# Replacing a hand-placed instruction order by a build-time list scheduler in a fused memory-attention and gated-MLP kernel

## The chip, the cores and the metric

The kernel runs on one core of one Trainium2 chip. The metric is device time in microseconds (us). The profile records the span from the first to the last instruction, which in these runs is 1.7 us shorter than the time. Engine names: PE is the TensorE matmul unit, PEld its weight loads, DVE is VectorE, ACT is ScalarE, POOL is GpSimd, SP is the engine that here only issues DMAs. The program gives each engine its own list of instructions; "order" in this text means the order of that list, engine by engine. That an engine keeps to it shows in the trace of the kernel before: from 95.71 to 96.65 us DVE stood idle, waiting for an ACT result, although the matmuls of two k groups were done at 94.4 us and only had to be copied out by DVE; these copies came later in its list.

An execution has a state, fast or slow (slow when it is more than 1.5% above the fastest of its kernel).

## The reference, cut to what matters

The input x is 2048 tokens of 512 values, in four segments of 512 tokens. Two branches read it and a gate per token mixes them.

```python
g = sigmoid((x * gate_w).sum(-1))                       # one gate per token
# branch A: 32 heads of 16, causal softmax inside each segment, plus a memory of earlier segments
for s in range(4):
    p = softmax(q_s k_s^T / 4 + causal_mask); a_dot = p @ v_s
    a_mem = (phi(q_s) @ M) / (phi(q_s) @ z + 1e-6)      # phi(t) = t + 1 if t > 0 else exp(t)
    o_s = sigmoid(beta) * a_mem + (1 - sigmoid(beta)) * a_dot
    M += phi(k_s)^T v_s ; z += phi(k_s).sum(tokens)
a = concat(o) @ wo
# branch B: gated MLP, width 1792
b = (gelu(x @ w_gate) * (x @ w_up)) @ w_down
out = g * a + (1 - g) * b
```

## The kernel before: the parts that the argument touches

There are three stages. First the inputs load and segment 0's k, q and v are computed. Then the gate matmuls of the MLP run with Gelu on ACT. Then comes the logit stage: 80 "logit slots" (4 segments, 4 chunks of 8 heads, 5 slots each). Each slot is a few small matmuls into two of three PSUM buffers called `lg`, followed by two exps of 128x1024 on ACT. All other PE work is "filler" between slots: k, q and v of the next segment, up projections, down and output projections, the PV products (`pv`) and the memory. Each filler group uses one of only two PSUM buffers called `gen`, which an "evacuation" by DVE (or ACT) must empty before it can be used again. The kernel has no other PSUM (matmul result memory) buffers than these five, before and after the change.

The order of filler work is written by hand. A running total of nominal PE costs spreads it over the slots, and a queue `pend` hands out small DVE operations one at a time:

```python
def qk_group(s, c, which):                   # filler: one k or q group
    t = gen(which)
    ...4 matmuls into t...
    nc.vector.tensor_copy(dst, t[:, :])                          # evacuation, DVE
    if which == "k":
        nc.vector.tensor_scalar_mul(KO[...], dst, odd[:, :])     # kO: SBUF to SBUF, DVE

def phi(src, dst):                           # phi of a 128x1024 tile
    nc.scalar.activation(E, src, AF.Exp)
    nc.vector.tensor_scalar_max(Q1, src, 0.0)
    nc.vector.tensor_scalar_min(E, E, 1.0)
    nc.gpsimd.tensor_add(dst, E, Q1)                             # POOL, 2.15 us

# ... fillers of segments 1 and 2 (cut):
f += [fl(0, phi_k, s, 0)] + f_k(s + 1, 0) + f_num(s, 1) + f_q(s + 1, 0)
f += f_out(s - 1, 0) + f_num(s, 2) + f_m(s, 0) + f_v(s + 1) + f_out(s - 1, 1)
# ...
for t in range(NSLOT):                       # per segment
    logit_slot(s, t)
    target = total * (t + 1) / NSLOT
    while True:
        if pvq and pvq[0][0] <= g and not opened:
            pv_group(*pvq.popleft()[1:]); pump(1); continue
        if not fs or done >= target:
            break
        cost, opened, fn = fs.popleft()
        fn(); done += cost; pump(1)
```

At the start, the small operations on `beta` (`bps`, a matmul into a `gen` buffer, and `tb`, an ACT operation) come before everything else in program order, and the tiny transfers gw and beta are issued on ACT's queue right after wk.

The softmax here doesn't subtract the row's maximum and nothing guards it: scores larger than these inputs give would overflow.

## Time and profile before

Before: 336.63 us median over 15 runs (335.74 to 338.76).

| stage (from the profile) | us | length, us |
|---|---|---|
| start, up to the first gate matmul | 0 to 29.0 | 29.0 |
| gates, up to the first exp | 29.0 to 93.7 | 64.7 |
| logit stage, first exp to end of last exp | 93.7 to 325.0 | 231.3 |
| tail | 325.0 to 337.3 | 12.3 |

These lines are from the profile page of the kernel before: the span, each engine's busy time, and the span in 40 equal slices, where each digit is the busy share in tenths (PEclk is the clock granted to PE).

```profile
span 337.3 us, 5732 instructions
PE 291.8 (87%) x2297; PEld 120.0 (36%) x2297; DVE 224.4 (67%) x425; ACT 200.0 (59%) x208; POOL 121.3 (36%) x186
PE   1389999999949997896899799869979998999963
DVE  1265354455585889789766886995787698456473
ACT  0122555344466786786478487828785686797840
PEclk9999999999987999999599899969998999999999
```

No engine is full throughout the last 70% of the span, although PE looks nearly so. The Trainium skill, "Perfetto Trace Analysis", section "Identifying the Most-Contended Engine", says that matmul busy share is not a good measure of how close PE is to its limit. This trace agrees: PE's busy time is larger than what its instructions need, as the next view shows. It gives the busy time of each engine in the logit stage of the kernel before; after the length come PE, PEld, DVE, ACT and POOL, then granted clock, DMA share and GB/s.

```profile
core 0: us, PE busy (x) PEld busy (x) DVE busy (x) ACT busy (x) POOL busy (x), PEclk, DMA share, GB/s
93.73:325.02 231.29, 206.87 (x1914) 83.22 (x1912) 174.32 (x330) 165.16 (x172) 114.84 (x171) 0.94 0.06 15
```

PE is "busy" for 207 us here, but the same instructions need about 187 us at full clock (an estimate: columns streamed at the trace's 0.216 us per 512, plus 0.1 us for each change to or from the small packed matmuls). The granted clock of 0.94 says where part of the difference lies.

The timeline of the start of the kernel before; columns are start, duration, engine, line, operation, output<-inputs, count, and in brackets the idle time before it and what ended it.

```profile
6.57 0.46 ACTq L89 DMA_DIRECT2D wq<-in_A_wq_dram  x1
12.64 1.28 ACT L184 ACT_TABLE_LOAD   x1 [12.64 <-DMA xT<-in_A_x_dram]
13.93 0.17 ACT L184 ACTIVATE tb<-bps 128x4 f32<-128x4 f32 x1
14.15 1.87 PE L150 MATMUL k<-xT,wk 128*128 128x512 bf16 x4 [5.37 <-ACT tb L184]
```

PE waited 5.4 us for `tb`, which held one of the two `gen` buffers, and ACT reached `tb` only after it had issued all its weight loads. The four matmuls then took 1.87 us; they began 0.43 us apart, where later ones begin 0.216 us apart.

The timeline of two stalls early in the logit stage of the kernel before:

```profile
96.99 0.69 DVE L157 CAST kT<-k 128x512 bf16<-128x512 f32 x1
97.22 2.12 POOL L330 TENSOR_TENSOR pkT<-E,Q 128x1024 bf16<-128x1024 bf16 x1 [1.07 <-issue]
97.71 1.78 DVE L161 TENSOR_SCALAR kO<-kT,odd 128x512 bf16<-128x512 bf16 x1
97.73 1.02 PE L150 MATMUL q<-xT,wq 128*128 128x512 bf16 x4 [3.35 <-DVE kT L157]
99.41 0.68 DVE L157 CAST kT<-k 128x512 bf16<-128x512 f32 x1
100.14 1.86 PE L150 MATMUL q<-xT,wq 128*128 128x512 bf16 x4 [1.05 <-DVE kT L157]
```

`kO` takes 0.35 us alone (at 100.12 in the same trace). Here it took 1.78 us and ended at 99.49, just after POOL's add ended at 99.34. The Trainium skill, "SBUF — State Buffer", section "Who interferes with whom", says that certain DVE operations and POOL exclude each other for a whole instruction; the trace agrees with that. The second kT evacuation waited behind it, and PE waited 1.05 us for the evacuation. The longer stall just before, 3.35 us, has nothing to do with POOL: the first kT evacuation stood in DVE's list behind phi's operations, and these waited for phi's exp, which ACT reached only at 95.56, after two exps of logits. At about 98.95 us the granted clock fell to 0.50 (1.00 in the window 98.8 to 98.9, 0.50 in 99.0 to 99.1), and the four matmuls at 100.14 took 1.86 us instead of 1.02. The second stall began only at 99.09, so it was not the one that brought the clock down here.

Three lines of the list of waits of the kernel before (who waited for whom: us in total, times, longest) show PE's largest wait and what such waits do to ACT:

```profile
PE q L150 <- DVE kT L157: 5.3, 6, 3.3
ACT pT L280 <- PE lg L276: 33.2, 44, 2.5
ACT pT L280 <- PE lg L269: 22.2, 11, 6.3
```

ACT, which needs about 155 us for the 160 exps (an estimate from the 1.94 us that two take back to back), waited 55 us for logits. PE itself waited 22.9 us for DVE evacuations in the logit stage (the sum of its lines in that list).

### The profile page before, as it was taken

The page shows a single profiled execution, that of the slowest core. Times are in us where ns is not written, and L with a number is a line of the kernel's source. Part 1 is how long each engine was busy: PE and PEld are TensorE (multiplying, and loading weights), DVE is VectorE, ACT ScalarE, POOL GpSimd, SP SyncE. Part 2 cuts the span into 40 slices and gives each one's busy share as a digit, 9 for nine tenths or more (in the row PEclk, how much of TensorE's full clock was granted, in tenths as well). Part 3 has the DMA queues.
Part 4 walks back from the last instruction along what each step waited for, and adds up shares of the span by engine and source line. Part 5 has one row for each costly group of instructions (what it writes and reads, how often), then busy time and mean ns, then how long its engine had stood idle before and what let it go on. Part 6 is the DMA issues. An engine that isn't in the chain of part 4 may idle for free.

```text
span 337.3 us, 5732 instructions
## 1 busy us (share of the span) xinstructions
PE 291.8 (87%) x2297; PEld 120.0 (36%) x2297; DVE 224.4 (67%) x425; ACT 200.0 (59%) x208; POOL 121.3 (36%) x186
## 2 busy tenths in 40 slices
PE   1389999999949997896899799869979998999963
PEld 0034444444413443342243343314424343334321
DVE  1265354455585889789766886995787698456473
ACT  0122555344466786786478487828785686797840
POOL 6000000000045345555255564346464533454520
PEclk9999999999987999999599899969998999999999
DMA  7999400000000001000100100010010000000001
GB/s 141 241 272 342 157 1 0 2 0 0 2 16 16 3 0 33 2 2 2 31 16 4 46 16 17 1 33 17 2 31 18 32 2 2 16 17 31 4 2 63
DMA packets 23108, 13.75 MB, mean 41 GB/s; under 512 B 16168, under 2 KB 22056, under 8 KB 23080
## 3 DMA queue, kind: packets, MB, share of 16 engines
q1 hardware_dynamic: 20400, 9.97, 10.9%
q10 hardware_dynamic: 2680, 3.41, 3.5%
q8 instruction: 18, 0.29, 0.4%
q14 instruction: 10, 0.08, 0.1%
HBM read 7.60 MB, written 2.10 MB: 29 GB/s over the span
## 4 chain that ended last, share of the span: by engine, by line
PE 65%; DVE 22%; ACT 5%; SPq 2%; issue 2%; DMA 2%; ACTq 0%; POOLq 0%; POOL 0%; DVEq 0%
PE gt L211 14%; PE up L175 14%; PE out L402 9%; PE lg L276 5%; PE v L166 4%; PE q L150 4%; PE dn L402 3%; PE pv L300 3%; DVE kO L161 3%; PE out L407 3%; DVE T L307 2%; DVE kT L157 2%; SPq L84 2%; DVE osb L425 2%; ACT pT L280 2%
## 5 line engine op out<-in xcount | busy, mean ns | idle before, releaser
L280 ACT ACTIVATE pT<-lg 128x1024 bf16<-128x1024 f32 x160 | 153.4, 1024 | 56.2 <-PE lg L276 33.2
L287 POOL TENSOR_SCALAR_AFFINE_SELECT pT<-pT 128x512 bf16<-128x512 bf16 (+1 forms) x160 | 90.1, 568 | 180.1 <-ACT pT L280 179.4
L175 PE MATMUL up<-xT,wup 128*128 128x512 bf16 x224 | 56.8, 388 | 1.9 <-DVE G L178 1.4
L178 DVE TENSOR_TENSOR G<-up,G 128x512 bf16<-128x512 f32 x56 | 38.3, 686 | 21.2 <-PE up L175 20.4
L215 ACT ACTIVATE G<-gt 128x1024 bf16<-128x1024 f32 x28 | 28.7, 1024 | 38.4 <-PE gt L211 38.4
L211 PE MATMUL gt<-xT,wga 128*128 128x512 bf16 x224 | 51.0, 379 | 0.0
L402 PE MATMUL out<-wdn,G 128*128 128x512 bf16 x168 | 42.6, 392 | 0.8 <-DVE T L307 0.8
L211 PEld LDWEIGHTS <-wga 128*128 128x128 bf16 x224 | 21.9, 98 | 26.5
L175 PEld LDWEIGHTS <-wup 128*128 128x128 bf16 x224 | 20.8, 99 | 29.3 <-issue 8.6
L402 PEld LDWEIGHTS <-G 128*128 128x128 bf16 x224 | 20.3, 101 | 29.4 <-issue 11.6
L300 PE MATMUL pv<-pT,vz 128*32 128x256 bf16 (+2 forms) x640 | 24.6, 281 | 4.7 <-DVE kT L157 3.2
L150 PE MATMUL q<-xT,wq 128*128 128x512 bf16 x64 | 22.0, 486 | 7.6 <-DVE kT L157 5.3
L150 PE MATMUL k<-xT,wk 128*128 128x512 bf16 x64 | 19.5, 440 | 10.0 <-ACT tb L184 5.4
L216 DVE TENSOR_TENSOR G<-G,g1b 128x1024 bf16<-128x1024 bf16 x28 | 19.0, 686 | 10.1 <-ACT G L215 10.1
L425 DVE CAST osb<-out 128x512 bf16<-128x512 f32 x12 | 8.2, 685 | 26.2 <-PE out L407 26.2
L307 DVE STREAM_TRANSPOSE T<-pv 128x512 f32<-128x512 f32 x32 | 22.9, 714 | 4.1 <-PE pv L300 4.0
L300 PEld LDWEIGHTS <-vz 128*32 128x32 bf16 x640 | 12.9, 98 | 16.7 <-issue 6.9
L330 POOL TENSOR_TENSOR pq<-E,Q 128x1024 bf16<-128x1024 bf16 x6 | 12.9, 2156 | 15.3 <-DVE E L329 15.3
L330 POOL TENSOR_TENSOR pkT<-E,Q 128x1024 bf16<-128x1024 bf16 x6 | 12.9, 2155 | 8.1 <-DVE E L329 7.1
L166 PE MATMUL v<-wv,xT 128*128 128x512 bf16 x64 | 15.3, 379 | 0.4 <-DVE r L312 0.4
L150 PEld LDWEIGHTS <-wk 128*128 128x128 bf16 x64 | 6.5, 107 | 25.1 <-issue 21.4
L150 PEld LDWEIGHTS <-wq 128*128 128x128 bf16 x64 | 6.7, 110 | 23.9 <-issue 20.3
(78 smaller groups left out, 292.2 us busy)
## 6 DMA issues: line engine op xcount, KB each, us to landing
out_dram<-osb SPq DMA_DIRECT2D x16, 128.0 KB, 1.7
wga<-in_B_w_gate_dram ACTq DMA_DIRECT2D x1, 1792.0 KB, 9.4
wup<-in_B_w_up_dram SPq DMA_DIRECT2D x1, 1792.0 KB, 7.7
wdn<-in_B_w_down_dram SPq DMA_DIRECT2D x1, 1792.0 KB
wk<-in_A_wk_dram ACTq DMA_DIRECT2D x1, 512.0 KB, 4.3
wq<-in_A_wq_dram ACTq DMA_DIRECT2D x1, 512.0 KB, 4.3
wv<-in_A_wv_dram ACTq DMA_DIRECT2D x1, 512.0 KB, 4.8
wo<-in_A_wo_dram SPq DMA_DIRECT2D x1, 512.0 KB, 13.1
```

What stands on the lines that cost most here:

```text
L150: nc.tensor.matmul(t[:, :], lhsT=W[:, fc, c * P:(c + 1) * P], rhs=xT[:, fc, s * L:(s + 1) * L], start=(fc == 0), stop=(fc == FC - 1))
L166: nc.tensor.matmul(t[:, :], lhsT=xT[:, fc, s * L + kt * P:s * L + (kt + 1) * P], rhs=wv[:, fc, :], start=(fc == 0), stop=(fc == FC - 1))
L175: nc.tensor.matmul(t[:, :], lhsT=wup[:, fc, hs * P:(hs + 1) * P], rhs=xT[:, fc, s * L:(s + 1) * L], start=(fc == 0), stop=(fc == FC - 1))
L178: nc.vector.tensor_mul(G[:, s, hs, :], t[:, :], G[:, s, hs, :])
L211: nc.tensor.matmul(t[:, i, :], lhsT=wga[:, fc, hs * P:(hs + 1) * P], rhs=xT[:, fc, s * L:(s + 1) * L], start=(fc == 0), stop=(fc == FC - 1))
L215: nc.scalar.activation(g, t[:, :, :], AF.Gelu_apprx_tanh)
L280: nc.scalar.activation(pt[:, :, :], A[h][:, :, :], AF.Exp, scale=0.25)
L287: nc.gpsimd.affine_select(out=v, in_=v, pattern=pat, compare_op=ALU.is_ge, fill=0.0, base=0, channel_multiplier=-1)
L300: nc.tensor.matmul(t[32 * j:32 * j + 32, qb * P:(qb + nq) * P], lhsT=vz[s % 2][:, kt, h * VW:h * VW + 32], rhs=pT[(s, c, w, j // 2)][:, j ...
L307: nc.vector.transpose(T[:, :, :].rearrange("p a b -> p (a b)"), t[:, :])
L330: nc.gpsimd.tensor_add(dst[:, :, :], E[:, :, :], Q1[:, :, :])
L402: nc.tensor.matmul(t[:, :], lhsT=G[:, s, hs, qt * P:(qt + 1) * P], rhs=wdn[:, hs, :], start=(hs == 0), stop=stop and (hs == HS - 1))
```

## The change

Intent: work out the order at build time by simulating the engines with a table of costs, rather than by hand. Every operation becomes a task with an engine (or a choice of engines), a cost in ns, dependencies, a priority, and the ring buffers it takes and frees. The scheduler repeatedly picks the engine that can start something first and, on that engine, the ready task of best priority. The chosen order is then emitted. Nothing is decided on the chip. The core of the diff:

```diff
+LAT = {"PE": 220, "ACT": 130, "DVE": 130, "POOL": 150, "SP": 0, "EXT": 0}
+MM = 216
+SWITCH = 100
+PACE = 1900
+        while n < len(self.tasks):
+            best = None
+            for e in ready:
+                c = [(w, t) for t in ready[e] for w in [when(t, e)] if w is not None]
+                ...
+                t0 = max(free[e], min(w for w, _ in c))
+                now = [(w, t) for w, t in c if w <= t0 + 1]
+                w, t = min(now, key=key)                      # priority, then program order
+                if best is None or t0 < best[0]:
+                    best = (t0, e, t)
+            assert best is not None, "no task can start"
+            ...
+            t.fn(e)                                           # emit on engine e
```

Other parts come with it:

```diff
     load_w(nc.scalar, wk, A_wk)
-    nc.scalar.dma_start(gw[:, :], ...)
-    nc.scalar.dma_start(beta8[:, :], ...)
     load_x(0)
     load_w(nc.scalar, wq, A_wq)
     load_w(nc.scalar, wv, A_wv)
+    nc.scalar.dma_start(gw[:, :], ...)
     load_w(nc.scalar, wga, B_w_gate)
+    nc.scalar.dma_start(beta8[:, :], ...)
+    warm = lgtile("warm")
+    for i in range(13):                                      # matmuls on zeros during the load
+        nc.tensor.matmul(warm[:, 0, :], lhsT=zbd[:, 0:P], rhs=zbd[:, 0:L], start=True, stop=True)
...                                                          # bps/tb behind segment 0's gates
+        AE = ["DVE", "ACT"]                                  # k, q, v, out evacuations: either engine
...                                                          # pv: both halves joined
-        pend.append(lambda: nc.vector.reciprocal(r[:, :, :], T[:, :, DH:DH + 1]))          # per half
+            nc.vector.reciprocal(RR[key][:, :, :, :], TT[key][:, :, :, DH:DH + 1])         # both
...                                                          # segment 3: down and output fused,
-            for qt in range(1, 4):                           # behind the last logits
-                f += f_down(3, qt)
+    for qt in range(KT):
+        last_group(NSEG - 1, qt, 1e4 + qt)
```

The matmuls are the same except for the 13 on zeros.

## The prediction

> **What bounds it now.** The page: span 337.3 us, PE 87% busy, DVE 67%, ACT 59%, chain 65% PE and 22% DVE. Stages, from the 10 us windows and the timeline:
> - 0 to 29 us, start. The chain runs x transposes, ACT table load (12.6), `tb` (13.9), then most k groups: ACT sat behind its own weight issues (wq leaves at 6.6, wv at 11.2), and `bps`, in one of two "gen" PSUM buffers, waited for it. k matmuls took 0.45 us each against 0.216 later: half clock of a PE not busy long enough (Trainium skill, "TensorE: Matmul & The Clock Gate", Part 1; the trace agrees).
> - 29 to 91 us, gates: PE 100% busy at 0.216 us a matmul. Only an earlier start helps.
> - 91 to 323 us, 80 logit slots of 2.9 us. Two exps take 1.94 us back to back: ACT needs 155 us plus 11.5 for phi. PE needs about 187: 167 of streaming (instructions by columns, logits and PV four abreast, 0.216 us per 512) and some 200 changes of packing at the 0.1 us the timeline shows. So 232 us are 81% filled. The rest is hand-placed order: PE waits for DVE (PE 7.2 and 7.5 us busy in 150-160 and 220-230), and after such gaps the clock falls (0.66 in 160-170 and 220-230).
> - 323 to 337 us, tail: four short projections.
>
> **What the change does.** A build-time list scheduler replaces the hand order.
> 1. Start: 13 warm matmuls during the load, `tb` behind the first gates, gw after wq and wv. k begins near 8 us at full clock; 12 groups at 0.86 to 1.04 us end near 20. Gates start near 20, not 29: minus 8 to 9 us, all on the chain.
> 2. Gates: same PE work, about 62 us; ends near 83.
> 3. Logit stage: 16 PSUM evacuations go to ACT at 0.6 us, taking 11 us off DVE; the halves' reciprocals and multiplies are joined (96 small ops, 29.8 us, become 48, about 21). DVE falls to about 162 us here. By the instruction order, three and a half of segment 3's four down groups move behind the last logits: streaming falls 167 to 153 us, with switches about 172. ACT needs about 155+11.5+10 = 176. PE and ACT are nearly equal, 2.2 us a slot; I expect 90 to 95% filling, 185 to 194 us, not more: DVE ops that meet POOL run longer than the scheduler's costs (kO 0.82 us mean, 0.35 alone; costed 0.40), and three logit and two gen buffers absorb little.
> 4. Tail: 20.7 us of streaming, not 5.4, plus 4 to store: 24 to 26, not 14.
>
> Sum: 83 + 1 + 188 + 25 = **297 us** (range 284 to 314). Faster by over 2%: 0.94; within 2%: 0.04; slower: 0.02.
>
> **What would show it.** Right: first gate matmul at 19 to 22 us; first exp at 83 to 86; last exp 270 to 277; granted clock near 1.0 after the start; ACT's wait for logits down from 55 us to under 25; tail near 25. Step 1 wrong: gates wait for wga (DMA above 0.9 past 22 us). Step 3 wrong: PE waits for DVE, slots of 2.6 us or more, low-clock slices remain.
>
> **What would make it wrong.** A static order is as good as its costs: if DVE runs later than planned, in-order engines stall each other, giving 310 to 325. If costs fit well, 97% filling gives 288.

## The result and the profile after

The changed kernel takes 296.46 us median (295.87 to 297.27, 12 runs), against 336.63 us. The ratio is 0.8796, with a 95% interval of 0.8777 to 0.8815. Ratios in this document are the mean time of one kernel's fast runs over that of the other's fast runs of the same rounds, so they are not quite the ratio of the medians.

| stage | before, us | predicted, us | after, us |
|---|---|---|---|
| first gate matmul at | 29.0 | 19 to 22 | 20.6 |
| first exp at | 93.7 | 83 to 86 | 85.5 |
| logit stage | 231.3 | 185 to 194 | 184.2 |
| end of last exp at | 325.0 | 270 to 277 | 269.7 |
| tail | 12.3 | 24 to 26 | 24.6 |
| span | 337.3 | 297 (said of the time) | 294.3 |

The page of the changed kernel, the same lines:

```profile
span 294.3 us, 5684 instructions
PE 278.6 (95%) x2310; PEld 118.9 (40%) x2310; DVE 200.5 (68%) x357; ACT 206.7 (70%) x224; POOL 126.1 (43%) x186
PE   6999999999999979999998999998999999998994
DVE  0664555555577798987999778689977964868400
ACT  0116655344379987899998899899998999895111
PEclk9999999999999999999999999999999999999999
```

There is no low-clock slice left, and ACT is above 80% in nearly all of the logit stage. The logit stage of the changed kernel in the view by windows (columns as before):

```profile
85.50:269.65 184.15, 176.25 (x1834) 74.10 (x1834) 151.37 (x263) 168.84 (x183) 119.62 (x171) 1.00 0.07 18
```

PE is busy 176 of 184 us and ACT 169. The stage is 47 us shorter with about the same ACT work. PE's busy time fell by 31 us, of which the moved down groups are about 15 (70 of the 224 down matmuls now run behind the last exp, at 0.216 us each); the rest is mostly the clock, 0.94 before and 1.00 after. PE's idle time in the stage fell from 24.4 to 7.9 us. The waits of the changed kernel:

```profile
ACT pT L521 <- PE lg L500: 12.3, 33, 1.8
PE pv L549 <- POOL pT L530: 1.8, 1, 1.8
```

ACT's wait for logits fell from 55 to 12 us. All waits of PE for another engine in the logit stage add up to 6.4 us.

The start of the changed kernel in the timeline:

```profile
1.95 5.06 PE L277 MATMUL warm<-zbd 128*128 128x512 bf16 x13 [1.95 <-DVE zbd L273]
8.95 3.17 PE L318 MATMUL k<-xT,wk 128*128 128x512 bf16 x13 [0.25 <-DMA xT<-in_A_x_dram]
20.59 9.66 PE L318 MATMUL gt<-xT,wga 128*128 128x512 bf16 x44
```

PE goes from the first data to the gates without a wait over 0.3 us. The end of the changed kernel:

```profile
274.80 3.18 PE L751 MATMUL dn<-wdn,G 128*128 128x512 bf16 x14
276.58 0.71 DVE L593 STREAM_TRANSPOSE xT<-N 128x512 bf16<-128x512 bf16 x1
290.58 0.60 ACT L176 ACTIVATE osb<-dn 128x512 bf16<-128x512 f32 x1 [3.29 <-PE dn L756]
```

The tail is twice as long as before, but PE works in it: the down group at 274.8 covers the time in which DVE finishes the last attention output at 277.3.

### The profile page after: what moved, and what is told of

Read it like the earlier page. It is cut to its first block, busy times and chain, and to the rows that moved or that the text cites. A ratio compares the mean times of both kernels' runs of the same rounds, so it can differ in the third digit from the quotient of the medians.

```text
span 294.3 us, 5684 instructions
## 1 busy us (share of the span) xinstructions
PE 278.6 (95%) x2310; PEld 118.9 (40%) x2310; DVE 200.5 (68%) x357; ACT 206.7 (70%) x224; POOL 126.1 (43%) x186
## 4 chain that ended last, share of the span: by engine, by line
PE 74%; DVE 20%; DMA 1%; SPq 1%; issue 1%; ACT 1%; ACTq 0%
PE gt L318 16%; PE dn L751 15%; PE up L318 14%; PE lg L500 6%; PE pv L549 6%; PE dn L756 4%; PE q L318 3%; PE v L356 3%; PE k L318 3%; DVE T L567 3%; DVE G L420 2%; DVE Nm L740 2%; DVE N L585 2%; DMA xT<-in_A_x_dram 1%; SPq L234 1%; DVE Tm L736 1%
## 5 line engine op out<-in xcount | busy, mean ns | idle before, releaser
L521 ACT ACTIVATE pT<-lg 128x1024 bf16<-128x1024 f32 x160 | 153.5, 1028 | 12.9 <-PE lg L500 12.3
L530 POOL TENSOR_SCALAR_AFFINE_SELECT pT<-pT 128x512 bf16<-128x512 bf16 (+1 forms) x160 | 94.3, 600 | 137.7 <-ACT pT L521 137.1
L751 PE MATMUL dn<-wdn,G 128*128 128x512 bf16 x224 | 53.6, 380 | 1.4 <-DVE T L567 1.3
L318 PEld LDWEIGHTS <-wup 128*128 128x128 bf16 x224 | 20.0, 97 | 25.8 <-issue 5.6
L549 PE MATMUL pv<-pT,vz 128*32 128x256 bf16 (+2 forms) x640 | 23.4, 275 | 3.0 <-POOL pT L530 1.8
L176 ACT ACTIVATE osb<-dn 128x512 bf16<-128x512 f32 x9 | 5.4, 596 | 19.0 <-PE dn L756 19.0
L500 PE MATMUL lg<-qT,kO 32*128 32x128 bf16 (+2 forms) x320 | 18.1, 272 | 0.0
L500 PE MATMUL lg<-qT,kT 16*128 16x256 bf16 (+2 forms) x320 | 18.0, 274 | 0.0
L318 PE MATMUL k<-xT,wk 128*128 128x512 bf16 x64 | 16.0, 379 | 2.0 <-DMA xT<-in_A_x_dram 1.0
L318 PE MATMUL q<-xT,wq 128*128 128x512 bf16 x64 | 16.3, 380 | 0.8 <-DVE kT L178 0.5
L756 PE MATMUL dn<-wo,xT 128*128 128x512 bf16 x64 | 16.5, 380 | 0.0
L622 POOL TENSOR_TENSOR pkT<-E,Q 128x1024 bf16<-128x1024 bf16 x6 | 13.5, 2257 | 3.6 <-DVE E L618 2.1
```

Of the source, the lines that this page charges most:

```text
L318: nc.tensor.matmul(t, lhsT=W[:, fc, c0:c0 + P], rhs=xT[:, fc, s * L:(s + 1) * L], start=(fc == 0), stop=(fc == FC - 1))
L500: nc.tensor.matmul(A[j // 2][:, j % 2, at * P:(at + nq) * P], lhsT=l, rhs=r, start=True, stop=True, tile_position=(32 * j, 0))
L521: nc.scalar.activation(pT[(s, t, h)][:, :, :], A[h][:, :, :], AF.Exp, scale=0.25)
L530: nc.gpsimd.affine_select(out=v, in_=v, pattern=pat, compare_op=ALU.is_ge, fill=0.0, base=0, channel_multiplier=-1)
L549: nc.tensor.matmul(t[32 * j:32 * j + 32, qb * P:(qb + nq) * P], lhsT=vz[s % 2][:, kt, h * VW:h * VW + 32], rhs=pT[(s, t0 + w, j // 2)][:, ...
L751: nc.tensor.matmul(t[:, :], lhsT=G[:, s, hs, qt * P:(qt + 1) * P], rhs=wdn[:, hs, :], start=(hs == 0), stop=stop and (hs == HS - 1))
```

## The experiments

The question after a forecast that came true is whether it came true for its reasons. The theory, called "order": the start is a separate saving of about 8 us, and nearly all the rest comes from where work is placed, that is, from PE no longer waiting for evacuations. Rivals, each of them another possible cause: the lighter DVE load (ACT evacuations, joined operations); the work moved behind the last logits; one specific repair (the kO collisions with POOL, or evacuations being given priority).

In the table, "equivalent" is the measured ratio times 336.6 us, so that runs of different sessions compare. The 95% intervals of these ratios are about plus or minus 0.005 (1.7 us), 0.008 for b_all_stt; the difference of two of them is uncertain by 2 us or more. The medians of the kernel before were 336.6 to 338.7 us in these sessions. The edits below are abridged: `...` and lines in words stand for code that is left out.

| kernel | ratio | equivalent, us | PE waits for other engines in logit stage, us | logit stage, us |
|---|---|---|---|---|
| before | 1 | 336.6 | 22.9 | 231.3 |
| b_start | 0.9767 | 328.8 | (profile slow) | |
| b_start_light | 0.9720 | 327.2 | 24.8 | 226.5 |
| b_all | 0.9763 | 328.6 | 25.7 | 220.9 |
| b_all_phi | 0.9632 | 324.2 | 25.5 | 216.0 |
| b_all_stt | 0.9771 | 328.9 | 26.8 | 221.0 |
| a_dve80 | 0.9122 | 307.1 | 14.2 | 196.4 |
| a_nolight | 0.9025 | 303.8 | 13.5 | 185.9 |
| a_noprio | 0.8905 | 299.7 | 9.1 | 190.5 |
| a_stt | 0.8839 | 297.5 | 7.5 | 181.7 |
| a_lock | 0.8830 | 297.2 | 8.3 | 187.7 |
| a_nowarm | 0.8803 | 296.3 | 6.4 | 184.2 |
| after | 0.8796 | 296.1 | 6.4 | 184.2 |
| a_meas | 0.8773 | 295.3 | 4.9 | 180.2 |

Kernels named b_ keep the hand order; those named a_ keep the scheduler. All gave correct results.

### Up from the kernel before: three parts of the change in the hand order

**b_start.** The kernel before with the start of the change.

```diff
-    load: wk, gw, beta, x0, wq, wv, wga, x1, x2, x3, wup, wdn, wo
+    load: wk, x0, wq, wv, gw, wga, beta, x1, wup, x2, x3, wdn, wo
+    for i in range(13): nc.tensor.matmul(warm..., lhsT=zbd..., rhs=zbd...)
-    bps/tb/omg/ebr/bdeb before everything; gate_row(0) between k and q
+    beta_part() after segment 0's gates; gate_row(0) after v; gwB copies after the first q
```

> The kernel before, hand order kept, with only the start of the change: new order of the input loads, 13 warm matmuls, the beta part behind segment 0's gates, the gate row after v. If the start is an independent saving, the first exp comes 8 to 9 us earlier (near 85 us, from 93.7), the logit stage and the tail stay as they were, and the time is 327 to 330 us. If the earlier start is eaten later (by waits for wga or wup, or in the logit stage), the time is 333 us or more.

Measured: 328.77, 329.23 and 330.42 us in the fast runs, ratio 0.9767. The run that was profiled fell into a slow state (418.84 us, mean granted clock 0.65), so its trace is not used for stages. The two kernels below contain the same start; their first exps come at 86.6 and 85.6 us. The start is worth 7.8 us (5.9 to 9.8 by the interval), about what the first exp gained, so little of it can have been lost later.

**b_start_light.** In addition, the lighter DVE load.

```diff
+        if which == "k" and s > 0 and c % 2 == 0: nc.scalar.activation(dst, t, AF.Copy)
-        nc.vector.tensor_copy(dst, t)
+        if qt % 2 == 0: nc.scalar.activation(osb, t, AF.Copy)     # out groups
-    per half: reciprocal, multiply by G2, multiply into N
+    once for both halves, on T of [P, 2, QB, 32]
```

The run also takes over the changed kernel's SBUF buffer counts (a larger T, the denominator's transpose moved to Tm, Nm in 3 buffers instead of 4), so these are no remaining difference between b_all and the changed kernel.

> As b_start, plus the lighter VectorE load of the change in the hand order: reciprocals and multiplies of the two halves joined, every second out group and every second k group of later segments evacuated by ACT. Theory 'order': the stalls come from where VectorE and PE work is placed, so less VectorE work alone gives 2 to 8 us, 320 to 327 us. Rival 'VectorE load': most of the logit stage's gain comes from it, and the time falls to 312 us or less.

Measured: 327.86 us, ratio 0.9720, that is 1.6 us below b_start, within the intervals. The rival "DVE load" falls: in the hand order that load is worth almost nothing, slightly less than even the 2 us at the low end of what "order" had expected. DVE's busy time in the logit stage did fall, from 174 to 163 us. But PE's waits only changed their cause: those for DVE fell from 22.9 to 16.6 us, and 8.2 us of waits for the evacuations that had been given to ACT came in, because these now stand between exps in ACT's list.

**b_all.** In addition, three of segment 3's four down groups go behind the last logits, fused with the output projection.

```diff
-            for qt in range(1, 4): f += f_down(3, qt)
     for qt in range(KT):
         t = gen("fin")
+        if qt: down(t, NSEG - 1, qt, 0, HS, False)
-        proj_o(t, NSEG - 1, qt, True)
+        proj_o(t, NSEG - 1, qt, qt == 0)
...                                          # these three are evacuated by ACT
```

> As b_start_light, plus three of segment 3's four down groups fused with the output projection behind the last logits, as in the change. Theory 'order': this only moves 9 us of PE streaming from the logit stage to the tail, so the time stays within 4 us of b_start_light, with the tail 9 to 10 us longer. Rival 'tail': a lighter logit stage is what makes it shorter, and the time falls by 8 us or more.

Measured: 329.49 us, ratio 0.9763. The logit stage became 5.6 us shorter than in b_start_light and the tail 8.6 us longer (13.4 to 22.0). The rival "tail" falls.

So three parts of the change, put into the hand order, give 8 of the 40 us. Two lines of the waits of PE in the logit stage of b_all, for two of the evacuations by ACT:

```profile
PE q L152 <- ACT kT L160: 2.8, 1, 2.8
PE num L404 <- ACT osb L440: 2.7, 3, 0.9
```

The logit stage of b_all in the view by windows (columns as before):

```profile
85.64:306.53 220.89, 194.03 (x1872) 78.50 (x1870) 162.18 (x270) 170.00 (x184) 115.27 (x171) 0.96 0.06 15
```

ACT's work is the same as in the changed kernel (170.0 and 168.8 us), DVE has 11 us more, and the stage is 37 us longer. The remaining difference from b_all to the changed kernel, 328.6 to 296.1, is 32.5 us. In the traces the two stages differ by 36.7 us: PE is idle 19.0 us less in the changed kernel (26.9 and 7.9) and busy 17.8 us less. About 6 of these 17.8 us are 28 further down matmuls that run behind the last exp there; the rest goes with the clock, 0.96 and 1.00.

### Down from the changed kernel

**a_nolight.** The scheduler stays, the lighter DVE load goes.

```diff
-        AE = ["DVE", "ACT"]
+        AE = ["DVE"]
-        ev = add(["DVE", "ACT"], [610, 560], fn, ...)
+        ev = add(["DVE"], [610], fn, ...)
-    r, rg, n: one task each for both halves (280, 120, 650 ns)
+    r, rg, n: one task each per half (200, 120, 370 ns)
```

> The changed kernel, its scheduler kept, but every PSUM evacuation on VectorE and the halves' reciprocals and multiplies separate again, as before the change (VectorE about 20 us busier). Theory 'order': the scheduler places the extra work too, and the time is 299 to 308 us. Rival 'VectorE load': 316 us or more.

Measured: 304.77 us, ratio 0.9025, 7.7 us slower. The scheduler with the old DVE load (start and tail of the change included) still takes 32.8 us off the time. Against b_start, which has the old DVE load too, it is 25.0 us faster. The light load is worth 7.7 us with the scheduler and 1.6 us, within the noise, without: it pays when the order lets it. PE was idle 13.6 us of the logit stage instead of 7.9. The loss shows mostly in the tail (31.8 us instead of 24.6), because the scheduler kept the logits going and let 6 us more of PE work slide behind them (PE is busy 26.7 us there instead of 20.4).

**a_noprio.** The priorities are ignored on DVE.

```diff
-                    return (p, t.seq)
+                    return (p, t.seq) if e != "DVE" else (w, t.seq)   # first ready, first served
```

> The changed kernel with the scheduler's priorities ignored on VectorE alone: there it takes operations in the order in which they become ready. If the priority of PSUM evacuations over the rest is what keeps PE fed, the time rises by 8 us or more; if the placement of PE work by modelled times does it, by less than 4 us.

Measured: 300.36 us, ratio 0.8905, 3.7 us slower. That is just under the 4 us line that had been drawn, but with an uncertainty of 2 us it is not clear of it. The logit stage itself is 6.3 us longer, of which the tail gives 2.4 back. So DVE's priorities are a smaller part of the 32.5 us. That the placement at modelled times does the rest is what the expectation concludes from this; the run alone does not show it, since the priorities on the other engines stayed.

**a_dve80.** Only the model is worse: the scheduler believes that DVE is faster than it is.

```diff
-            cost = t.engs[e]
+            cost = t.engs[e] * (0.8 if e == "DVE" else 1)
```

> The changed kernel with a worse model only: the scheduler believes every VectorE operation takes 0.8 of what it is told. If the order is as good as its costs, PE waits for evacuations again and the time rises by 4 to 12 us. If any sensible greedy order does, it rises by less than 2 us.

Measured: 307.57 us, ratio 0.9122, 11 us slower, with PE's waits up from 6.4 to 14.2 us. Factors of 0.5, 0.6 and 0.7 could not be tried: the scheduler stopped with "no task can start", because tasks that ran early in the model had taken ring buffers that the others needed. With costs that are too low the order gets worse; a_meas below tries higher ones.

### What the hand order did wrong

**b_all_phi.** One thing moved in b_all: phi of k after the k groups.

```diff
-f += [fl(0, phi_k, s, 0)] + f_k(s + 1, 0) + ...
+f += f_k(s + 1, 0) + [fl(0, phi_k, s, 0)] + ...        # and likewise in the other three places
```

> b_all (hand order with the change's start, lighter VectorE and tail; 329.5 us) with one thing moved: phi of k is emitted after the two k groups and their kO, not before them, so that POOL's 2.15 us add no longer runs while kO does. If hand-placed collisions of kO with POOL (kO 0.89 us mean there, 0.40 in the changed kernel) are a main cause of the stalls, kO falls to about 0.4 us, the low-clock slices thin out and the time falls by 6 to 14 us. If the cause is spread over many places, it falls by less than 4 us.

Measured: 325.49 us, ratio 0.9632, 4.4 us faster than b_all, between the two expectations. These are the lines of the groups table for kO, first in b_all and then in b_all_phi; after the first bar stand the busy time in us and the mean in ns of one.

```profile
L166 DVE TENSOR_SCALAR kO<-kT,odd 128x512 bf16<-128x512 bf16 x16 | 14.2, 889 | 0.5
```

```profile
L166 DVE TENSOR_SCALAR kO<-kT,odd 128x512 bf16<-128x512 bf16 x16 | 5.9, 366 | 2.9 <-ACT kT L160 2.5
```

The collisions of kO are gone, and so is nearly all of the low clock: the logit stage of b_all_phi by windows:

```profile
85.99:301.97 215.98, 187.46 (x1843) 77.54 (x1870) 156.28 (x270) 169.62 (x184) 116.48 (x171) 0.99 0.06 15
```

Yet only 4.4 of the 32.5 us came back, and PE's waits for evacuations did not shrink (25.7 and 25.5 us). PE's busy time fell by 6.6 us (part of that may be 29 PE records fewer in this trace), its idle time rose by 1.7 us, and the stage became 4.9 us shorter. So what came back has the size of the loss to the low clock, and the waits stayed, spread over other evacuations. The edit moves all of phi, its exp on ACT included, so it does not separate the collisions from the waiting behind phi that the stall of 3.35 us showed.

**b_all_stt.** POOL's add removed from b_all.

```diff
-        nc.vector.tensor_scalar_min(E, E, 1.0)
-        nc.gpsimd.tensor_add(dst, E, Q1)
+        nc.vector.scalar_tensor_tensor(out=dst, in0=E, scalar=1.0, in1=Q1, op0=ALU.min, op1=ALU.add)
```

> b_all with phi's add taken off POOL: one VectorE operation does min and add, no other order changes. All VectorE operations are then free of POOL's long adds (kO near 0.4, N+Nm near 0.45 us) but VectorE does 0.3 to 0.7 us more per phi. If collisions with POOL make most of the 33 us between b_all and the changed kernel, the time falls to 308 us or less; if order makes it, it stays at 316 us or more.

Measured: 329.19 and 330.92 us in the fast runs, ratio 0.9771, no different from b_all; the other two runs, 334.60 and 335.06 us, were slow ones. kO fell to 0.42 and N+Nm to 0.54 us, but the new operation takes 1.23 us on DVE. PE's waits stayed at 26.8 us. The rival "POOL collisions" falls as the main cause, unless the new DVE time hid some 20 us of gain, which the 1.6 us for the lighter DVE load makes unlikely. As this edit swaps one DVE load for another, it does not say what the collisions alone cost; neither does b_all_phi, as said.

### What is left, and an attempt to beat the changed kernel

The largest wait of PE that is left looks like this in the timeline of the changed kernel:

```profile
106.38 2.12 POOL L622 TENSOR_TENSOR pkT<-E,Q 128x1024 bf16<-128x1024 bf16 x1
106.48 2.57 DVE L585 TENSOR_TENSOR N<-T,r 128x512 bf16<-128x512 f32 x1
109.71 0.73 PE L549 MATMUL pv<-pT,vz 128*32 128x512 bf16 x20 [1.77 <-POOL pT L530]
```

A DVE operation that takes 0.69 us alone (at 275.39) met POOL's add, PE's evacuations waited behind it, and the masking on POOL waited behind the add. The scheduler knows nothing of such meetings. Three kernels tried to use that.

**a_stt.** The same fusion of min and add as above, in the scheduled kernel, with its cost given as 1.15 us.

> The changed kernel with phi's min and add done by one VectorE operation instead of two operations on VectorE and POOL, and the scheduler told so (1.15 us). If the PE gaps that are left are those where a VectorE operation met POOL's add (N<-T,r took 2.57 us at 106.5 and PE waited 1.8 us), 3 to 8 us come off: 288 to 293 us. If VectorE is what fills up in those stretches, the added VectorE time costs as much as it saves: 295 to 300 us.

Measured: 298.64 us, ratio 0.8839, 1.4 us slower. The logit stage is 2.4 us shorter (181.7), the tail 4.5 us longer. From the first exp on DVE is busy 155.6 us, against 156.2 in the changed kernel: the new operation takes about as much DVE time as the collisions and the removed operation did.

**a_lock.** The scheduler is told of the exclusion, in one direction: such a DVE operation may not start during POOL's add, but the add may start during the operation. Operations and costs are unchanged.

```diff
+            if e == "DVE" and t.lock and port[0] <= max(w, free[e]) < port[1]:
+                w = port[1]              # port: start and end of POOL's latest phi add
```

> The changed kernel, the same operations, but the scheduler is told that VectorE operations with two SBUF inputs, or on bf16 SBUF data alone, cannot start while POOL's 2.25 us phi add runs; it fills that time with PSUM evacuations and transposes. If the collisions seen in the changed kernel's trace (N<-T,r up to 2.57 us, N<-N,Nm up to 2.23 us against 0.4 to 0.7 alone) cause what is left of PE's waits for evacuations (about 6 us in the logit stage), the time falls by 2 to 5 us, to 291.5 to 294.5 us, and those two means fall to 0.75 and 0.5 us. If other small mismatches make up the rest, it stays within 1.5 us of 296.5.

Measured: 297.44 us, ratio 0.8830, slower by 1.1 us or the same within the intervals. The groups table says why this decides little. N<-T,r in the changed kernel and then in a_lock:

```profile
L585 DVE TENSOR_TENSOR N<-T,r 128x512 bf16<-128x512 f32 x16 | 14.8, 926 | 0.3
```

```profile
L591 DVE TENSOR_TENSOR N<-T,r 128x512 bf16<-128x512 f32 x16 | 14.7, 919 | 0.3
```

The mean did not fall, and that of N<-N,Nm did not either (0.79 and 0.81 us). Why is not shown: the model may keep the two apart by less than the chip strays from it, or the direction that it does not know may matter. The expectation about the means failed, so the run does not test what the collisions cost.

**a_meas.** The measured mean DVE costs, collisions included, in place of the given ones.

```diff
-    EV = {"DVE": 610, ...}; r 280; r*G2 120; N 650; N+Nm 500; xT 640; Nm 680; Mbd 620
+    EV = {"DVE": 640, ...}; r 330; r*G2 350; N 900; N+Nm 760; xT 670; Nm 720; Mbd 710
```

> The changed kernel with the scheduler's VectorE costs raised to the mean times that the changed kernel's trace shows, collisions with POOL included (N<-T,r 0.90 us instead of 0.65, N<-N,Nm 0.76 instead of 0.50, r<-r,G 0.35 instead of 0.12, an evacuation 0.64 instead of 0.61, and so on). If costs of a model are what is left to gain, the time falls to 292 to 295 us. If the given costs are already within what a static order can use, it stays within 2 us of 296.5, and no version of these beats the changed kernel.

Measured: 295.95 us (295.29 to 299.67 in the fast runs; a slow one took 301.25), ratio 0.8773 with an interval of 0.8720 to 0.8827, which contains that of the changed kernel. The logit stage is 4 us shorter and the tail 3.4 us longer. Here the collisions did become fewer (N<-T,r 0.80 us on average instead of 0.93, N<-N,Nm 0.55 instead of 0.79), and PE's waits fell from 6.4 to 4.9 us, and still the time stayed. No version tried beats the changed kernel beyond the noise.

The scheduler can also be run without the chip, with its costs alone (a calculation, not a run). Its own end time is then 293.7 us for the changed kernel (span 294.3), 294.5 for a_dve80 (span 305.1) and 301.8 for a_meas (span 294.3). So the 11 us of a_dve80 are time that its model did not foresee, and the close agreement for the changed kernel is partly luck: with the measured mean costs the model is 7 us too slow.

**a_nowarm.** One warm matmul instead of 13.

```diff
-    for i in range(13):
+    for i in range(1):
```

> The changed kernel with one warm matmul instead of 13. The first 3 to 4 us of real matmuls then run at 0.43 us instead of 0.216: 8 or so of the k group at half clock, 1.5 to 2.5 us lost before the gates, and the same at the end: 298 to 299 us. If VectorE's evacuations (1.04 us a k group) bound the k groups anyway, the loss is under 1 us.

Measured: 296.97 us, ratio 0.8803. The start in the timeline:

```profile
7.55 5.42 PE L318 MATMUL k<-xT,wk 128*128 128x512 bf16 x16 [4.99 <-DMA xT<-in_A_x_dram]
```

The 16 k matmuls took 5.42 us instead of about 4.3 (7.78 to 12.12), and the first gate came 0.9 us later (21.5 instead of 20.6). So did the first exp, and the profiled span is 0.9 us longer; the medians of the times differ by 0.5 us, and by the intervals a loss of up to 1.7 us is possible. Warm matmuls are a small part of the start's 7.8 us; the 1.5 to 2.5 us expected before the gates were too many, and the other branch, under 1 us, came true. The Trainium skill, "TensorE: Matmul & The Clock Gate", Part 1, describes the half clock before 3.4 us of activity, and the trace shows it: from 7.55 to 10.92 us the matmuls begin 0.43 us apart, from 11.3 us on 0.216. (The view by windows reads a granted clock of 1.00 all that while, so at the start the spacing is the better witness.) In the changed kernel, though, the k groups wait for their evacuations on DVE (the third and the fourth begin 0.99 us apart, where four matmuls need 0.86) and for x, so the clock was only part of their pace.

## Why the prediction was right, point by point

1. **Start, minus 8 to 9 us.** First gate at 20.6 instead of 29.0 us in the traces; the start alone in the hand order gave 7.8 us (b_start). Right in size. The weight that the text put on "full clock" was too high (a_nowarm: 0.9 us in the trace). By elimination the rest is moving `tb` and `bps` and the load order; these were not separated from each other.
2. **Gates, same PE work, about 62 us.** 20.6 to 85.5 us with PE busy 64.7 of 64.9 us. Right; first exp within the range given.
3. **Logit stage, 188 us, limited by PE and ACT nearly equally.** 184.2 us, just under the range of 185 to 194, and the last exp ended 0.3 us before its range. Both are above 91% busy. In place of the three and a half down groups named, 70 down matmuls, as many as five groups have, run behind the last exp: four groups of segment 3 and one of segment 2. That is 15 us of streaming, close to the 14 us that the prediction had taken off. The terms were a little off in both directions: PE busy 176 us against 172 estimated; ACT 169 against 176, since 5 of the 16 ACT evacuations fall in the tail and operations back to back overlap a little (two exps of 1.02 us take 1.94); DVE 151 against about 162. Part of the DVE miss is in the sum itself: 174 us less the two savings named, 11 and 9, is 154. Another part is kO: 13.1 us in the kernel before, 6.3 us after, where its longest one takes 0.77 us instead of 1.78. The prediction had named kO as the operation that would hold the scheduler back; in its place N<-T,r (0.93 us on average, 0.69 alone) and N<-N,Nm (0.79, 0.4 alone) collide.
4. **Placement as the cause.** The prediction gave the fill of the stage (81% to 90 or 95%) as the main gain without proving that order causes it. The runs support this: three parts of the change in the hand order give 8 of 40 us; the scheduler with the start and the tail of the change but without the light load gives 33. Which engine evacuates is part of what the scheduler decides in the changed kernel; a_nolight takes that freedom away and keeps most of the gain. PE's waits for evacuations go 22.9, 25.7 (b_all), 6.4 us, and ACT's waits for logits 55, 44 and 12 us.
5. **Tail of 24 to 26 us.** 24.6 us. Right.
6. **The sum.** 297 was a sum of spans. The span became 294.3 us, 2.7 less: the logit stage 3.8 and the tail 0.4 us less, the first exp 1.5 us later than the 84 of the sum. The time includes 1.7 us outside the span. That the sum met 296.5 so closely is partly luck: these differences cancel.
7. **What would make it wrong.** A model whose DVE costs are 20% too low costs 11 us (a_dve80). That is in the direction named, though smaller than the 13 to 28 us given there.

What stays open: how the 32.5 us between b_all and the changed kernel divide among single placements. One (phi before k) is 4.4 us. PE's waits for evacuations differ by 19 us, which is also what its idle time differs by; the rest is lower clock and work that slid behind the last logits. Waits and low clock go together in these traces, and no run separates how much of the clock the waits cost.

## What to carry to other kernels

When several in-order engines are each 60 to 90% busy and wait for each other through a few buffers, sum what each engine needs and compare the largest sum with the stage: here 187 us needed in 231 said what a better order could give, before any edit. The lighter DVE load paid little (1.6 us, within the noise) while the order was wrong, and 7.7 us afterwards. A build-time scheduler with uncontended start-to-start costs got within about 10 us of the engines' own needs (184 us for the stage, PE 176 of them busy). Its DVE costs should not be too low: 20% cost 11 us here, while measured means that include the collisions brought nothing clear of the noise.

## What the Trainium skill lacked or had wrong

- "TensorE: Matmul & The Clock Gate", Part 1, knows half and full clock, 13/16 when three cores of a die run dense matmuls, and a clock seen stuck at 1/4. One run of b_start, of a program on one core, fits none of these: its granted clock was 0.63 to 0.65 in every stretch after the first 20 us, and it took 418.84 us instead of 329; 14 gate matmuls took 4.76 us (0.34 us each). Why is not known.
- "SBUF — State Buffer", "Who interferes with whom", has the exclusion of DVE and POOL right, but not what it costs behind the DVE operation: kO at 1.78 instead of 0.35 us held an evacuation and left PE idle for 1.05 us.
